# Attention and two expert stages on one core: attention's PSUM and the opening order rearranged

## The chip, the core and the metric

The kernel runs on one core of a Trainium2 chip. The engines of the core that matter here are TensorE (PE in the profile; PEld is its weight load), VectorE (DVE), ScalarE (ACT), GpSimd (POOL) and the queue engine SyncE (SP). [...] The metric is the device time of one execution, in microseconds (us).

## What is computed

Attention over 4 batches, 8 heads and 768 positions, in chunks of 32 queries that see 8 memory keys and a window of their neighbours; then a mixture of 8 experts whose weights come from a balanced softmax over all 3072 tokens; then one more feed-forward stage.

```python
def _attn_ref(q, k, v, mem_k, mem_v):            # q, k, v: (4, 8, 768, 64)
    for c in range(S // 32):                     # keys c*32-16 .. c*32+40, cut at 0 and S
        scores = scale * q_c @ concat(mem_k, k_ctx).T
        a = exp(scores - max(scores)); a = a / (sum(a) + 1e-9)
        out[c] = a @ concat(mem_v, v_ctx)

def _moe_ref(x, w_gate, w1, w2):                 # x: (3072, 512), w1: (8, 512, 1024)
    P = exp(x @ w_gate - max)
    for _ in range(8):
        P /= P.sum(1) + 1e-9; P /= P.sum(0) + 1e-9; P *= N / E
    return sum(P[:, e] * (relu(x @ w1[e]) @ w2[e]) for e in range(8))

def _moe2_ref(x, w_in, w_out):                   # w_in: (512, 2048)
    return relu(x @ w_in) ** 2 @ w_out
```

## The kernel before, in words

Every fp32 operand of a product is scaled by a power of two and split into a high and a low fp16 half; a product is then three fp16 products (low by high, high by low, high by high). ACT makes the high half, DVE or POOL the low one by a subtraction.

Attention works on 32 tiles of 96 queries. One tile goes through these steps (functions `a_...`): load k, v, q into one of three buffers `raw`; `a_scale`, `a_all`, `a_row_max`, `a_spread`, `a_scale2` find the largest magnitude of each of the three and make scales of it (L247 to L271; two tiny products on PE in between); `a_split` and `a_split_lo` make the halves (L300 on ACT, L305 on DVE); `a_tqk` turns q and k by a transposing DMA on SP's queue (L310); `a_scores` computes the scores (L329, L341), `a_max` their row maxima (L350 to L355, DVE); `a_mt`, `a_mtc` turn the maxima (L361 on PE, L367 on ACT); `a_st` computes the scores a second time, turned and with the maximum taken off (L378, L381); `a_exp` (L390), `a_asplit` (L396), `a_asplit_lo` (L402, POOL) make the weights; `a_av` (L411 to L419) multiplies with v; `a_norm` (L428 to L431, DVE) divides; `a_xsplit`, `a_xsplit_lo` split the result and `a_tx` turns it into `xt` by transposing DMAs (L455). `setup_less` builds three mask tables `less` on ACT (L1462, L1465), which the scores need.

Expert 0 runs in between: token blocks of 128, 128 and then 256 tokens; for a block `l1_mm` computes x @ w1 (L784 to L786, a group of 24 products for each quarter f of the hidden columns), `l1_relu` on ACT (L791) and `l1_lo` on DVE (L796) make the halves of the result, `l2_part` multiplies with w2 (L1291 to L1293), `l2_acc` stores (L1299). Its weights are loaded by SP (`w1_load0` L581, `w2_load0` L587), searched for their maximum by DVE (L590), scaled and split by ACT (L652, L655) and POOL (L658). The gate products (`gate` L465, L472 and `gate_out` L482) run once for each 128 tokens. After the last tile and gate `open_post` opens the pools of the later stages; experts 1 to 7 and the last stage follow with products at L930 and L1291.

PSUM during attention: four one-bank buffers `sc` (two for each of the two score steps), two banks `ps` for the experts, and one two-bank tile `avb`. `avb` holds the output of `a_av` in both banks and, behind it in the second bank (`mmb`), the small results of `a_all`, `a_spread`, `a_mt` and `gate`.

The order of the work on every engine is computed when the program is built: the class `Plan` takes tasks with an engine, a cost, a priority and what they wait for, and always places the task that can start first (ties by priority). Its rings stand for buffers; `lane` stands for 8 semaphores that all DMAs share in turn, so that a DMA waits for the one eight before it. Each engine then runs its list strictly in that order.

Of the kernel before, what the change touches and what calls it, by code (L numbers as in the profile page):

```python
# [7 lines left out]
F32 = mybir.dt.float32  # L8
# [13 lines left out]
    "hi": 1.85, "lo": 2.25, "tqk": 3.1, "scores": 0.95, "max": 1.65, "mt": 0.12, "mtc": 0.25,  # L22
    "st": 1.0, "exp": 1.05, "ahi": 0.85, "alo": 1.7, "av": 0.8, "norm": 1.05, "xhi": 0.65,
    "xlo": 0.7, "tx": 1.25,
}
LAND = {"load": 1.8, "tqk": 4.4, "tx": 1.7, "w": 2.5}
SLACK = 0.6
MOVE = {"load": 3.6, "tqk": 4.5, "tx": 1.5, "w1": 1.5, "w2": 1.3}
X2 = [[[0, 3, 5, 8], [9, 10, 14, 17], [1, 4, 13, 15, 10, 15, 21]], [[0, 3, 5, 8], [9, 10, 14,
# [24 lines left out]
def tile_attention_moe_moe2(  # L54
# [92 lines left out]
    ident16 = ap_.tile([TQ, TQ], F16, name="ident16")  # L147
# [11 lines left out]
    avb = psa.tile([P, 2, 512], F32, name="avb")  # L159
    mmb = avb[:, 1, 4 * VP:]  # L160
# [47 lines left out]
    def a_load(i):  # L208
# [3 lines left out]
        dq = nc.sync if i in (0, 2) else nc.scalar  # L212
        hd = lambda ap: ap.rearrange("p (h d) -> p h d", h=H)
        for t, src, mem in ((1, k, mem_k), (2, v, mem_v)):
            lo, hi = s0 - LEFT, s0 + TQ + RIGHT
# [5 lines left out]
            if c0 > lo:  # L221
# [9 lines left out]
            if mem_in.get((raw_of(i), t)) != b:  # L231
# [3 lines left out]
                )  # L235
        dq.dma_start(
# [6 lines left out]

    def a_scale(i):
        raw = raws[raw_of(i)]
        mx = ap_.tile([P, 3], F32, tag="amx", name="amx", bufs=2)
        nc.vector.tensor_reduce(mx, raw, AX.X, ALU.max, apply_absolute_value=True)  # L247
        st[i, "amx"] = mx

    def a_all(i):  # L250

        p = mmb[0:3, 0:P]
# [8 lines left out]
    def a_spread(i):  # L261
        p = mmb[:, P:P + 3]
# [5 lines left out]
    def a_scale2(i):  # L268
        sc, inv = pow2(st.pop((i, "gm")), 3, T_QKV, sml, "a")
        sce = sml.tile([P, 1], F32, tag="sce", name="sce", bufs=6)  # L270
        nc.vector.scalar_tensor_tensor(  # L271
            sce, inv[:, 0:1], 1.0 / float(D) ** 0.5, inv[:, 1:2], ALU.mult, ALU.mult
        )
        st[i, "sc"], st[i, "sce"], st[i, "inv"] = sc, sce, inv

    def a_invx(i):
        inv = st.pop((i, "inv"))
        t0 = i * TQ
        while t0 < (i + 1) * TQ:
# [3 lines left out]
            nc.gpsimd.tensor_copy(invx[p0:p0 + n, c:c + 1], inv[p0:p0 + n, 2:3])  # L283
# [28 lines left out]

    def qk_of(qkT, h):
# [10 lines left out]
    def a_scores(i):  # L324

        qkT = st[i, "qkT"]
        scs = [psa.tile([TQ, 4, P], F32, tag="sc", name="sc", bufs=4) for u in range(2)]
# [15 lines left out]
        st[i, "scp"] = scs  # L343

    def a_max(i):

        scs = st.pop((i, "scp"))
        mx = ap_.tile([TQ, 2, 4], F32, tag="smx", name="smx", bufs=2)
        for g in range(2):
# [3 lines left out]
        m = mx.rearrange("p g h -> p (g h)").unsqueeze(1).to_broadcast([TQ, 2, H])  # L353
# [3 lines left out]
    def a_mt(i):  # L357

        p = mmb[0:MR, P + 4:P + 4 + TQ]
        m16 = m16s[i % 2].rearrange("p g c -> p (g c)")[:, 0:MR]  # L360
        nc.tensor.matmul(p, lhsT=m16, rhs=ident16, start=True, stop=True)  # L361
# [8 lines left out]
    def a_st(i):  # L370

        qkT, mt = st.pop((i, "qkT")), st.pop((i, "mt"))
        scs = [psa.tile([P, 4, TQ], F32, tag="sc", name="sct", bufs=4) for u in range(2)]
# [10 lines left out]
        st[i, "scp"] = scs  # L384

    def a_exp(i):
        scs, sce = st.pop((i, "scp")), st.pop((i, "sce"))
        e = ap_.tile([P, H, TQ], F32, tag="e", name="e")
        for g in range(2):
            nc.scalar.activation(e[:, 4 * g:4 * g + 4, :], scs[g], AF.Exp, scale=sce)  # L390
# [13 lines left out]
    def a_av(i):  # L404
        aT = st.pop((i, "aT"))
        v16 = v16s[i % NV]
        o = avb[0:TQ]
# [53 lines left out]
    def gate(t):  # L461
        b, c = divmod(t * P, BLK)
        lgp = mmb[:, 228:228 + 2 * E].rearrange("p (s e) -> p s e", s=2)
        for kk in range(KD):
            nc.tensor.matmul(  # L465
                lgp.rearrange("p s e -> p (s e)"),
                lhsT=xt[b][:, 0, kk, c:c + P],
                rhs=g16[:, kk].rearrange("p s e -> p (s e)"),
                start=(kk == 0),
                stop=False,  # L470
            )
            nc.tensor.matmul(  # L472
# [1490 lines left out]
```

## Time and profile before

| | us |
|---|---|
| median of 3 runs (lowest, highest) | 2533.57 (2528.68, 2533.63) |
| the profiled execution, its own time | 2531.32 |
| its span from first to last instruction | 2529.5 |
| PE busy, share of the span | 2407.2, 95% |
| DVE busy | 1871.1, 74% |

The profile divides the span into 40 slices of 63 us. PE's busy share reads 2 tenths in the first slice, 6 in the second and 9 in each of the others. A row of the timeline gives the start, the duration and the instruction, and in brackets how long the engine stood idle before it and what ended that. A row of a table of stretches gives, for each engine, its busy time in the stretch.

### The profile page before, as it was taken

What the parts mean: (1) busy time and instruction counts of PE and PEld (TensorE: products, weight loads), DVE (VectorE), ACT (ScalarE), POOL (GpSimd) and SP (SyncE); (2) the same over time, 40 slices, a digit from 0 to 9 for tenths busy, and PEclk for the clock granted to TensorE, in tenths of its full rate; (3) what the DMA queues carried; (4) which work ended last, traced back from release to release, by engine and by line L of the source; (5) the groups of instructions that cost most, each with busy time, mean ns of one, the idle gap of its engine ahead of it and who ended that gap; (6) DMA issues with size and microseconds to landing.
All of it is one profiled execution on the core that took longest, in us unless ns stands there. A gap on an engine that the chain in (4) does not pass through costs nothing.

```text
span 2529.5 us, 54257 instructions
## 1 busy us (share of the span) xinstructions
PE 2407.2 (95%) x22483; PEld 2015.5 (80%) x22483; DVE 1871.1 (74%) x2759; ACT 1337.6 (53%) x2294; POOL 1327.3 (52%) x1108
## 2 busy tenths in 40 slices
PE   2699999999999999999999999999999999999999
PEld 1566666657678888888888888888888878888888
DVE  7788764856577887888788788977858987666655
ACT  4455543423345564555556555555656657666453
POOL 2221211443545574675567467555746677866444
PEclk9999999999999999999999999999999999999999
DMA  8699774223353445445344544533333466553211
GB/s 173 100 144 145 120 109 90 80 76 111 112 198 117 142 123 189 131 145 188 116 142 132 176 134 142 188 124 101 119 119 112 141 165 161 164 168 113 91 64 48
DMA packets 358656, 329.53 MB, mean 130 GB/s; under 512 B 237320, under 2 KB 292104, under 8 KB 351752
## 3 DMA queue, kind: packets, MB, share of 16 engines
q1 hardware_dynamic: 274792, 305.08, 41.5%
q10 hardware_dynamic: 83616, 20.98, 5.3%
q8 instruction: 176, 2.88, 0.5%
q14 instruction: 72, 0.59, 0.1%
HBM read 214.84 MB, written 77.07 MB: 115 GB/s over the span
## 4 chain that ended last, share of the span: by engine, by line
PE 82%; DVE 12%; ACT 2%; DMA 2%; issue 1%; POOL 1%; ACTq 0%; SPq 0%; DVEq 0%; POOLq 0%
PE pbA L930 36%; PE pbE L930 18%; PE pbB L930 8%; PE pb L930 4%; PE py L1291 3%; PE py L1292 3%; PE py L1293 3%; PE ph L784 1%; PE ph L786 1%; PE ph L785 1%; DVE hp L1128 1%; DVE acc L1241 1%; PE sc L341 1%; DVE smx L350 1%; PE sct L378 1%
## 5 line engine op out<-in xcount | busy, mean ns | idle before, releaser
L930 PEld LDWEIGHTS <-wb 128*128 128x128 f16 x5184 | 507.4, 98 | 68.0 <-issue 7.6
L930 PEld LDWEIGHTS <-hp 128*128 128x128 f16 x4608 | 450.9, 98 | 58.0 <-DVE hp L1128 3.0
L930 PEld LDWEIGHTS <-wx 128*128 128x128 f16 x3888 | 380.8, 98 | 52.8 <-issue 8.0
L930 PEld LDWEIGHTS <-xt 128*128 128x128 f16 x3456 | 338.2, 98 | 48.3 <-DVE xt L1128 7.3
L930 PE MATMUL pbA<-w2p,hp 128*128 128x256 f16 x2304 | 291.4, 273 | 3.7 <-DVE hp L1128 1.9
L930 PE MATMUL pbA<-S,wb 128*128 128x256 f16 x2304 | 283.3, 273 | 6.2 <-ACT u L1058 2.0
L930 PE MATMUL pbE<-xt,wx 128*128 128x256 f16 x2304 | 284.1, 273 | 4.7 <-DVE u L1063 3.8
L1058 ACT ACTIVATE u<-pbA 128x512 f32<-128x512 f32 x180 | 106.5, 592 | 186.5 <-PE pbA L930 186.5
L402 POOL TENSOR_TENSOR aT<-e,aT 128x768 f16<-128x768 f32 x32 | 53.0, 1657 | 228.9 <-ACT aT L396 152.0
L930 PE MATMUL pbA<-w2p,xt 128*128 128x256 f16 x1152 | 157.1, 273 | 0.0
L930 PE MATMUL pbE<-xt,hp 128*128 128x256 f16 x1140 | 156.6, 274 | 0.0
L930 PE MATMUL pbE<-xt,xt 128*128 128x256 f16 x1140 | 156.2, 273 | 0.2 <-POOL xt L1128 0.2
L1291 PE MATMUL py<-w2p,hp 128*128 128x512 f16 x384 | 147.6, 384 | 7.6 <-DVE hp L921 6.0
L1058 ACT ACTIVATE xt<-pbA 128x512 f32<-128x512 f32 x147 | 86.6, 592 | 128.0 <-PE pbA L930 128.0
L1128 POOL TENSOR_TENSOR hp<-u,hp 128x512 f16<-128x512 f32 x86 | 115.2, 1339 | 65.0 <-ACT hp L1121 65.0
L1292 PE MATMUL py<-w2p,hp 128*128 128x512 f16 x384 | 147.1, 383 | 0.0
L1293 PE MATMUL py<-w2p,hp 128*128 128x512 f16 x384 | 146.9, 383 | 0.0
L930 PE MATMUL pbA<-S,wx 128*128 128x256 f16 x1152 | 141.4, 273 | 2.3 <-ACT xt L1058 0.9
L930 PE MATMUL pbA<-xt,wb 128*128 128x256 f16 x1152 | 141.4, 273 | 0.0
L930 PE MATMUL pbB<-xt,wb 128*128 128x256 f16 x1152 | 141.4, 273 | 0.0
L1063 DVE TENSOR_TENSOR u<-pbE,u 128x512 f32<-128x512 f32 x100 | 68.6, 686 | 92.4 <-ACT u L1058 55.1
L1128 POOL TENSOR_TENSOR xt<-u,xt 128x512 f16<-128x512 f32 x72 | 94.8, 1325 | 54.9 <-ACT xt L1121 54.9
(367 smaller groups left out, 5710.6 us busy)
## 6 DMA issues: line engine op xcount, KB each, us to landing
wst<-in_moe_w_dram SPq DMA_DIRECT2D x80, 512.0 KB
xt<-xdr SPq DMA_DIRECT2D x40, 1024.0 KB
S<-sdr SPq DMA_DIRECT2D x126, 256.0 KB
w2d<-wst SPq DMA_DIRECT2D x32, 512.0 KB
w2p<-w2d SPq DMA_DIRECT2D x32, 512.0 KB
wst<-in_moe_w_dram SPq DMA_DIRECT2D x56, 256.0 KB
xdr<-xt SPq DMA_DIRECT2D x12, 1024.0 KB
w2d<-tw SPq DMA_DIRECT2D x32, 384.0 KB
```

The lines of the kernel that those rows point to most:

```text
L341: nc.tensor.matmul(scs[u][:, hh, :], lhsT=q_, rhs=k_, start=False, stop=(s == 2 and hh == 3))
L350: nc.vector.tensor_reduce(mx[:, g], scs[g], AX.X, ALU.max)
L378: nc.tensor.matmul(scs[u][:, hh, :], lhsT=k_, rhs=q_, start=(s == 0 and hh == 0), stop=False)
L402: nc.gpsimd.tensor_tensor(aT[:, 1], st.pop((i, "e")), aT[:, 0], ALU.subtract)
L784: nc.tensor.matmul(p[:, r], lhsT=w[:, 1], rhs=xh, start=first, stop=False)
L930: nc.tensor.matmul(p[:, r], lhsT=w[:, ws], rhs=x[:, xs], start=a, stop=z, skip_group_check=onto)
L1058: nc.scalar.activation(t, p, AF.Copy, scale=sc)
L1063: nc.vector.tensor_tensor(t, p, t, ALU.add)
L1128: eng.tensor_tensor(d[:, 1], t, d[:, 0], ALU.subtract)
L1291: nc.tensor.matmul(p, lhsT=h[:, 1], rhs=w[:, 0], start=first, stop=False)
L1292: nc.tensor.matmul(p, lhsT=h[:, 0], rhs=w[:, 1], start=False, stop=False)
L1293: nc.tensor.matmul(p, lhsT=h[:, 0], rhs=w[:, 0], start=False, stop=last)
```

## The change

- **PSUM by use.** `avb` goes. The scale steps get a bank of their own (`pa`), the row maxima and their turned form another (`pb`), and the two score steps, the output of `a_av`, the gate products and the new transposes share a ring of two two-bank buffers (`wide`, tag `sc`). The row maximum and the exponential become one instruction each over both banks; the scale steps and the maxima stay in PSUM while they are worked on.
- **Tiles 0 and 1** are turned by products with an identity on PE and copied out by ACT or DVE (`a_tq1`, `a_tqc`; 16 products of 128 columns a tile); the results x of tiles 0, 1 and 2 likewise (`a_tx1`, `a_txc`; 8 products a tile).
- **Loads.** Tiles 0 to 3 are loaded by SP's queue, except v of tile 0, which goes to ACT's; tile 1's loads stand ahead of most of the w1 loads. The rows of tile 0 ahead of position 0 are set to zero by DVE in place of being loaded.
- **Weights of expert 0**: one scaled ACT instruction and one DVE instruction in place of two on ACT and one on POOL; the L1 groups need only two of the four w1 pieces each, and run f = 0, 2, 1, 3.
- **Gates**: six groups of four token tiles; the gate weights are prepared after tile 16, the maxima of expert 1's w2 after tile 22.
- `a_invx` moves from POOL to ACT.
- **The plan** adds to a task's possible start an offset for its step (`AHEAD`) and a share of its priority by engine (`AGE`), and places the smallest sum first. Costs are renewed.

```diff
+AHEAD = {
+    "join": -0.54, "setup_less": 2.51, "a_all": -0.23, "a_row_max": -0.45, "a_spread": -0.08,
...
-        dq = nc.sync if i in (0, 2) else nc.scalar
+        dq = nc.sync if i < 4 else nc.scalar
...
+            if i == 0 and t == 2:
+                dq = nc.scalar
...
+    def wide(nm, rows=P):
+        return psa.tile([rows, 2, 512], F32, tag="sc", name=nm, bufs=2)
...
-        p = mmb[0:3, 0:P]
+        st[i, "pa"] = pa = psa.tile([P, 256], F32, tag="pa", name="pa", bufs=1)
+        p = pa[0:3, 0:P]
...
+        nc.vector.tensor_scalar(
+            eb.bitcast(I32), eb.bitcast(I32), EXP_MASK, None, ALU.bitwise_and)
+        nc.vector.tensor_scalar(inv, eb, 2.0 ** -100, 2.0 ** -T_QKV, ALU.max, ALU.mult)
+        nc.vector.tensor_scalar(eb, eb, 2.0 ** -100, None, ALU.max)
+        nc.vector.tensor_scalar(
+            sc.bitcast(I32), eb.bitcast(I32), -1.0, float((254 + T_QKV) << 23), ALU.mult, ALU.add)
...
-            nc.gpsimd.tensor_copy(invx[p0:p0 + n, c:c + 1], inv[p0:p0 + n, 2:3])
+            nc.scalar.activation(invx[p0:p0 + n, c:c + 1], inv[p0:p0 + n, 2:3], AF.Copy)
...
+    def a_tq1(i, m):
+        p = wide("sqt")
+        for c in range(8):
+            n = 8 * (c // 4) + 4 * m + c % 4
+            nc.tensor.matmul(
+                p[:, c // 4, c % 4 * P:(c % 4 + 1) * P], lhsT=st[i, "qk"][:, n * P:(n + 1) * P],
+                rhs=ident16, start=True, stop=True)
+        st[i, "tq", m] = p
...
-            nc.vector.tensor_reduce(mx[:, g], scs[g], AX.X, ALU.max)
+        st[i, "pb"] = pb = psa.tile([P, 128], F32, tag="pb", name="pb", bufs=1)
+        mx = pb[0:TQ, TQ:TQ + H]
+        nc.vector.tensor_reduce(mx, scs.rearrange("p g (h n) -> p (g h) n", h=4), AX.X, ALU.max)
...
-        o = avb[0:TQ]
+        o = wide("av", TQ)
...
+    def w_hi0(n, d):
+        nc.scalar.activation(flat(d[:, 0]), flat(stage0[n]), AF.Copy, scale=wsc[0, n // 4][0])
+
+    def w_lod0(n, d):
+        nc.vector.scalar_tensor_tensor(
+            flat(d[:, 1]), flat(stage0[n]), wsc[0, n // 4][0], flat(d[:, 0]), ALU.mult, ALU.subtract)
...
+        fill(raws[0][0:LEFT, 1:3, :], 0.0)
...
+                        key = t + AHEAD.get(fn.__name__, 0.0) + AGE.get(eng, 0.0) * pri / 100
...
-        plan = Plan({"lane": 8, "lgp": 1, "pmax": 1, "pall": 1, "pmt": 1, "sc": 4, "av": 1, "ps": 2})
+        plan = Plan({"lane": 8, "pa": 1, "pb": 1, "sc": 2, "ps": 2})
...
+            if blk and (c0 + n0) % (NGP * P) == 0:
+                t = (c0 + n0) // (NGP * P) - 1
+                G[t] = add("PE", 0.36 * NGP, 9000, gate, t, after=x_in + [W["gp"]], ring=("sc", 1))
...
-                w_in_ = [W["lo", n] for n in range(4)]
+                w_in_ = [W["lo", 2 * (f % 2) + n] for n in range(2)]
```

The order that the plans give, at three places. First ACT at the start of the program, before (`raw_162` and `raw_163` are the buffers of tiles 0 and 1, `qk` and `v` the high halves):

```order
L217 DMA raw_163<-in_k_dram 120x8x64
L233 DMA raw_163<-in_mem_k_dram 8x8x64
L217 DMA raw_163<-in_v_dram 120x8x64
L233 DMA raw_163<-in_mem_v_dram 8x8x64
L236 DMA raw_163<-in_q_dram 96x8x64
L1462 ACTIVATE less<-heads 83x1024
L1465 ACTIVATE less<-maskr 3x1024 x2
L300 ACTIVATE qk_298<-raw_162,asc 128x512 x2
L300 ACTIVATE v_0_165<-raw_162,asc 128x8x64
```

and the same engine now, from its first instruction (`sqt` is q and k turned by PE, in PSUM):

```order
L235 DMA raw_162<-in_v_dram 104x8x64
L251 DMA raw_162<-in_mem_v_dram 8x8x64
L1560 ACT_TABLE_LOAD
L1560 ACTIVATE less<-heads 83x1024
L1563 ACTIVATE less<-maskr 3x1024 x2
L360 ACTIVATE qk_293<-raw_162,asc 128x512 x2
L360 ACTIVATE v_0_164<-raw_162,asc 128x8x64
L317 ACTIVATE invx<-ainv 96x1
L381 ACTIVATE qkT<-sqt 128x2x512
```

All three mask tables and tile 1's five loads stood ahead of tile 0's high halves; now one table does, the other two stand behind, and tile 1's loads are on SP's queue.

Second, the low halves of expert 0's w1 (`wb`). Before, on POOL:

```order
L283 COPY invx<-ainv 96x1
L283 COPY invx<-ainv 32x1
L283 COPY invx<-ainv 64x1
L658 TENSOR_TENSOR wb_84<-acc_78,wb_84 128x1024
L658 TENSOR_TENSOR wb_86<-acc_78,wb_86 128x1024
L658 TENSOR_TENSOR wb_85<-acc_79,wb_85 128x1024
L658 TENSOR_TENSOR wb_87<-acc_79,wb_87 128x1024
L402 TENSOR_TENSOR aT<-e,aT 128x768
```

and now on DVE, between steps of tiles 2, 5 and 6 (`x_941` is the low half of tile 2's result, `qk_893` that of tile 5):

```order
L270 TENSOR_REDUCE amx<-raw_162 128x3
L517 TENSOR_SCALAR rs<-av 96x8
L518 RECIPROCAL rs<-rs 96x8
L520 TENSOR_TENSOR acc_83<-av,rs 96x512
L285 TENSOR_REDUCE ag<-pa 3x1
L754 SCALAR_TENSOR_TENSOR wb_84<-acc_78,w0sc,wb_84 128x1024
L534 TENSOR_TENSOR x_941<-acc_83,x_941 96x512
L339 SCALAR_TENSOR_TENSOR qk_893<-acc_83,asc,qk_893 128x512 x2
```

The four subtractions moved from POOL, where they ran ahead of the first tile's weights, to DVE, the first behind tile 2's division and the others further down.

Third, DVE behind the row maxima of tile 7, up to tile 6's division (`rs`). Before:

```order
L350 TENSOR_REDUCE smx<-sc 96x4 x2
L354 CAST m_1_159<-smx 96x2x8
L355 TENSOR_TENSOR m_1_159<-smx,m_1_159 96x2x8
L190 TENSOR_SCALAR aeb<-avb 128x3
L191 TENSOR_SCALAR ainv<-aeb 128x3
L194 TENSOR_SCALAR asc<-ainv 128x3
L271 SCALAR_TENSOR_TENSOR sce<-ainv 128x1
L590 TENSOR_REDUCE wmx<-acc_82 128x1
L247 TENSOR_REDUCE amx<-raw_163 128x3
L428 TENSOR_SCALAR rs<-avb 96x8
```

and now, from the fourth instruction behind the same maxima (`qk_1649` and `v_0_164` are tile 8's low halves, `pa` the scale steps in PSUM):

```order
L285 TENSOR_REDUCE ag<-pa 3x1
L339 SCALAR_TENSOR_TENSOR qk_1649<-acc_83,asc,qk_1649 128x512 x2
L339 SCALAR_TENSOR_TENSOR v_0_164<-acc_83,asc,v_0_164 128x8x64
L270 TENSOR_REDUCE amx<-raw_163 128x3
L300 TENSOR_SCALAR pa<-pa 128x3
L302 TENSOR_SCALAR ainv<-pa 128x3
L303 TENSOR_SCALAR pa<-pa 128x3
L304 TENSOR_SCALAR asc<-pa 128x3
L306 SCALAR_TENSOR_TENSOR sce<-pa,ainv 128x1
L285 TENSOR_REDUCE ag<-pa 3x1
L517 TENSOR_SCALAR rs<-av 96x8
```

Tile 8's low halves moved in between the maxima and the division, and the search of expert 1's w2 (`acc_82`) has gone from there.

## Rows read from the trace of the kernel before

**Rows 1.** The page: span, and PE's busy tenths in 40 slices.
```profile
span 2529.5 us, 54257 instructions
...
PE   2699999999999999999999999999999999999999
```
**Rows 2.** Stretches: length, busy (count) of PE, PEld, DVE, ACT, POOL, granted clock, DMA.
```profile
0.00:87.40 87.40, 26.79 (x352) 20.17 (x353) 66.88 (x139) 46.96 (x60) 31.36 (x51) 1.00 0.77 147
...
34.50:87.40 52.90, 25.09 (x345) 19.44 (x345) 45.84 (x85) 30.15 (x43) 25.09 (x19) 1.00 0.63 118
87.40:113.00 25.60, 17.71 (x209) 14.50 (x209) 11.38 (x22) 7.93 (x18) 2.12 (x4) 0.87 0.77 111
113.00:444.00 331.00, 312.50 (x3941) 218.68 (x3941) 236.99 (x503) 154.30 (x297) 62.35 (x78) 0.99 0.76 121
```
**Rows 3.** Timeline (start, us, instruction): tile 0 from the fills to its scores.
```profile
0.96 1.03 DVE L1421 MEMSET raw<- 32x512 f32 x2 [0.96 <-PEq L1947]
...
9.13 2.13 ACT L1465 ACTIVATE less<-maskr 3x1024 bf16<-3x1024 bf16 x2 [1.55 <-POOL maskr L1459]
...
18.77 1.33 ACT L300 ACTIVATE qk<-raw,asc 128x512 f16<-128x512 f32 x2
...
22.46 9.52 SPq L310 DMA_TRANSPOSE qkT<-qk  x2
...
34.55 0.66 PE L329 MATMUL sc<-less,onehot 3*96 3x512 bf16 x2
```
**Rows 4.** DVE groups by form, 0 to 88 us: count, busy us, mean ns, idle before.
```profile
L590 DVE TENSOR_REDUCE wmx<-acc 128x1 f32<-128x1024 f32 x8 | 9.4, 1204 | 0.0
L247 DVE TENSOR_REDUCE amx<-raw 128x3 f32<-128x1536 f32 x5 | 8.7, 1747 | 10.9 <-DMA raw<-in_q_dram 10.9
L350 DVE TENSOR_REDUCE smx<-sc 96x4 f32<-96x512 f32 x10 | 6.4, 677 | 2.2 <-PE sc L341 2.2
L305 DVE SCALAR_TENSOR_TENSOR qk<-raw,asc,qk 128x512 f16<-128x512 f32 x8 | 5.6, 744 | 0.0
...
L431 DVE TENSOR_TENSOR acc<-avb,rs 96x512 f32<-96x512 f32 x3 | 2.1, 686 | 0.1
```
**Rows 5.** Timeline: POOL's w1 halves, DVE's small steps beside and after; page's POOL group.
```profile
34.69 8.44 POOL L658 TENSOR_TENSOR wb<-acc,wb 128x1024 f16<-128x1024 f32 x4 [9.53 <-issue]
34.92 1.93 DVE L191 TENSOR_SCALAR ainv<-aeb 128x3 int32<-128x3 int32 x1
...
43.09 0.14 DVE L190 TENSOR_SCALAR aeb<-avb 128x3 int32<-128x3 int32 x1
43.34 0.17 DVE L191 TENSOR_SCALAR ainv<-aeb 128x3 int32<-128x3 int32 x1
...
L402 POOL TENSOR_TENSOR aT<-e,aT 128x768 f16<-128x768 f32 x32 | 53.0, 1657 | 228.9 <-ACT aT L396 152.0
```
**Rows 6.** Timeline: PE's two long stops around the first L1 groups, and ACT's.
```profile
87.38 0.31 PE L361 MATMUL avb<-ident,m 96*83 96x96 f16 x1 [4.67 <-DVE m L355]
...
105.23 0.18 ACT L482 ACTIVATE lg<-avb 128x16 f32<-128x16 f32 x1 [8.36 <-DMA acc<-in_v_dram]
...
105.47 0.21 PE L411 MATMUL avb<-v,aT 128*96 128x65 f16 x1 [6.90 <-ACT lg L482]
```
**Rows 7.** Timeline of PE: 12 L1 products, 24 later ones, tile 5's scores.
```profile
87.48 0.31 PE L784 MATMUL ph<-xt,wb 128*128 128x128 f16 x1
...
88.65 0.31 PE L786 MATMUL ph<-xt,wb 128*128 128x128 f16 x1
...
93.71 0.22 PE L784 MATMUL ph<-xt,wb 128*128 128x128 f16 x1
...
94.99 0.22 PE L786 MATMUL ph<-xt,wb 128*128 128x128 f16 x1
...
113.47 0.87 PE L341 MATMUL sc<-qkT 64*96 64x128 f16 x24
```
**Rows 8.** Timeline: end of one tile's last product with v, and its division on DVE.
```profile
193.27 0.21 PE L419 MATMUL avb<-v,aT 128*96 128x65 f16 x1
...
202.39 0.69 DVE L431 TENSOR_TENSOR acc<-avb,rs 96x512 f32<-96x512 f32 x1
```

More of the change, by code (lines that the diff above doesn't have):

```diff
@@ L235, in a_load @@
                 )
+        dq = nc.sync if i == 0 else dq
         dq.dma_start(
@@ L326, in a_scores @@
         qkT = st[i, "qkT"]
-        scs = [psa.tile([TQ, 4, P], F32, tag="sc", name="sc", bufs=4) for u in range(2)]
+        both = wide("sc", TQ)
+        scs = [both[:, u].rearrange("p (h n) -> p h n", h=4) for u in range(2)]
         for g, sc in zip(GRP, scs):
@@ L372, in a_st @@
         qkT, mt = st.pop((i, "qkT")), st.pop((i, "mt"))
-        scs = [psa.tile([P, 4, TQ], F32, tag="sc", name="sct", bufs=4) for u in range(2)]
+        both = wide("sct")
+        scs = [both[:, u, 0:4 * TQ].rearrange("p (h n) -> p h n", h=4) for u in range(2)]
         for s in range(3):
@@ L1575, in tile_attention_moe_moe2, with join, s_hi0, s_lo0 @@
         }
-        RING = {"row": ("pmax", 1), "all": ("pall", 1), "mt": ("pmt", 1), "scores": ("sc", 2),
-                "st": ("sc", 2), "av": ("av", 1), "tqk": ("lane", 1)}
-        FREE = {"row": ["row_mx"], "all": ["scale"], "mt": ["mtc"], "scores": ["max", "max"],
-                "st": ["exp", "exp"], "av": ["norm"]}
+        RING = {"row": ("pa", 1), "max": ("pb", 1), "scores": ("sc", 1), "st": ("sc", 1), "av": ("sc", 1),
+                "tqk": ("lane", 1)}
+        FREE = {"row": ["scale"], "max": ["mtc"], "scores": ["max"], "st": ["exp"], "av": ["norm"]}
         T = {}
-        LS = [add("ACT", 3.2, 5 + 100 * mv, setup_less, mv) for mv in range(3)]
+        def join():
+            pass
+        def s_hi0():
+            s_hi(*st["sf", 0])
+        def s_lo0():
+            s_lo(*st.pop(("sf", 0)))
+        S0 = add(None, 0.0, -999, join, land=6.0)
+        LS = [add("ACT", 3.2, 5 + 100 * mv, setup_less, mv, after=[S0]) for mv in range(3)]
         for i in range(NA):
@@ L1586, in tile_attention_moe_moe2 @@
                 eng = ENG[n]
-                if n == "load" and i in (0, 2):
+                if n == "load" and i < 4:
                     eng = "SP"
@@ new lines, in tile_attention_moe_moe2 @@
+                if n == "tx" and i < PX:
+                    lasts = []
+                    for m in range(2):
+                        tq = add("PE", 0.45, pri, a_tx1, i, m, after=after if m else [T[i, "xhi"]] + after[1:],
+                                 ring=("sc", 1))
+                        act = m == 0 or i > 0
+                        cp = add("ACT" if act else "DVE", 0.5, pri - 1, a_txc, i, m, act, after=[tq])
+                        holds(tq, cp)
+                        lasts.append(cp)
+                    T[i, "tx"] = add(None, 0.0, pri - 1, join, after=lasts, land=0.2)
+                    continue
```

216 lines of the change are left out of this document (145 added, 71 removed), and 3 rows, old and new, of the table AHEAD.

## Prediction

> **What bounds the kernel now.** I read the page first. PE is busy 95% of a span of 2529.5 us, and its slices read 2 and 6 tenths at the start and 9 from then on [rows 1]. So the kernel is bound by PE except in its opening, and since the change touches nothing behind attention and expert 0, its gain must come out of that opening. The table of stretches says how much is there: up to 87.4 us PE works 26.8, from 87.4 to 113 it works 17.7 of 25.6 at a mean clock of 0.87, and from 113 to 444, where attention and expert 0 run side by side, it works 312.5 of 331 [rows 2]. In the last of these only 18.5 us are open; in the first two 68.5 are, though part of that is the latency of the first tiles and cannot go.
>
> What holds the opening? From 34.5 to 87.4 DVE is busy 45.8 of 52.9 us and ACT 30.2 [rows 2]: DVE works its list without a gap worth naming, and the first L1 product, at 87.48, starts behind a small product that had waited 4.67 us for DVE [rows 6, 7]. Ahead of that the timeline of tile 0 shows a chain without load: mask tables on ACT until 11.26, more of them behind tile 1's loads, the high halves only at 18.77, a transposing DMA issued at 22.46, scores only at 34.55 [rows 3]. Behind it there is one long stop: PE idles 6.90 us up to 105.47 for a gate copy on ACT, which had stood 8.36 us behind a load that waited for its DMA semaphore [rows 6].
>
> **The change, part by part.**
>
> *Tile 0 to its scores.* The new fill of 16 x 1024 stands first on DVE; two fills of 32 x 512 take 1.03 us together, and so will this one [rows 3]. POOL's masks, and with them the one table that is still ahead of tile 0, end 1.0 us later: 9.13 + 2.13 + 1.0 = 12.3. High halves of k and q 1.33 (to 13.6), the three low halves on DVE 0.74 each behind the first of them (to 15.0). Then DVE's list has tile 1's maximum, 1.75 (to 16.7), ahead of the copy of the turned low halves. No row shows that copy; a reduction over 512 columns of PSUM takes 0.68, so 1024 cost about 1.3 [rows 4]: 18.0. PE's 16 turning products, 0.106 each as 128-column products at the lower of PE's two clock levels [rows 7], lie beside DVE's work. This needs tile 1 to have landed by 15; its loads are issued right behind tile 0's and one w1 piece. Scores of tile 0 at 18, not 34.55. If tile 1 lands at its old 19, the copy ends at 22: bounds 17 and 22.
>
> *From there to the first L1 product.* It needs two pieces of w1 and x of tiles 0 and 1. In the new list of DVE the low half of the second piece stands behind these, each with its row's duration [rows 4, 5]: 7 searches of weights 1.20 = 8.4; 6 maxima of inputs 1.75 = 10.5; 5 row maxima, two halves of 0.68 and two small steps = 8.5; 15 low halves 0.74 = 11.2; 30 scale steps 0.17 = 5.1; 4 divisions 0.69 + 0.35 = 4.2; 3 low halves of x 0.69 = 2.1; some 21 small steps 4.4; one copy 0.5; the two w1 halves, each twice a 0.74 = 3.0. Sum 57.9. Durations overlap a little from one to the next, and DVE also waits: in the old stretch 7.1 of 52.9 were not busy [rows 2]. I let the two nearly cancel: 18 + 58 + 1 = 77, bounds 74 and 84, against 87.48. PE's list ahead of it is by then through the turned scores of tile 4, and its waits fit into this.
>
> Not in that sum any more: the stretched steps. One scale step took 1.93 us while POOL ran its four w1 halves, and 0.17 undisturbed [rows 5]. POOL no longer has them, and the scale steps now read PSUM, as the one of 0.14 does. [...]
>
> *From the first L1 to the dense stretch.* PE's new list has 168 L1 products of 128 columns, two score steps, one turned score step and two products with v ahead of the first product with w2. Products start 0.106 apart for the first 6 us and 0.056 from 93.71 on [rows 7]: 57 x 0.106 + 111 x 0.056 = 12.3, and about 1.2 for each of the five attention steps, 18 in all: 95. DVE's list has 17 us of work from the second w1 half to the first w2 half and 22 to the fourth: 94 and 99. So products with w2 start at 95 and may wait for DVE up to 4 us. Before, tile 5's scores start at 113.47 with 96 L1 products of 128 columns and 15 w2 products of 512 issued [rows 7]; the new list at 95 is ahead of that point by 1536 columns or 0.6 us of expert work and by two score steps, one turned one and one product with v, about 4. The 6.90 stop is not repeated: the gates leave this place. Gain: 113.5 + 4.6 - 95 = 23, less 3 for DVE: **20**. From the bounds: 10 to 26.
>
> *The rest, 113 to 444.* Zero, and here is its cover. DVE gets 8 weight halves (12 us, half of them above) and one more scale step a tile (5 us), and is busy 237 of 331 [rows 2]. ACT gets POOL's copies of scales and loses eight passes over weights; it is busy 154 of 331. The gate products are the same 192, in six lumps. The gate weights and expert 1's maxima go behind tiles 16 and 22, where DVE has room, and expert 0's token tile 19 is what waits for the latter. The waits through `avb` in that stretch can give back at most what is open, 18.5. Against that the ring of two wide buffers is tighter, see below. Sum: 2531.32 - 20 = **2511**. The profiled execution lies inside the runs (2528.68 to 2533.63), so I give the same number for the median.
>
> **The rivals.**
>
> *DVE late once more.* w1's and w2's low halves now run on DVE with two operands in SBUF, while POOL subtracts for the attention weights, 1.66 us each [rows 5]. If DVE and POOL block each other where they meet, the six POOL instructions ahead of the first w2 product put up to 6 x 1.66 = 10 us into DVE's chain. The gain falls to 10: **2521**. For it: the 1.93 us step beside POOL. Against it: the plan lets these two kinds of work not overlap. It decides from about half of the meetings. [...]
>
> *The ring of two.* Scores, turned scores and products with v share two buffers, and PE works in order. In the new list the step two places after a product with v comes 2.6 to 5 us of PE work later; it must find that buffer divided and free. Before, the division ended 9.6 us after the product (193.48 to 203.08), at no cost, since that buffer was waited for by nobody else until the next one [rows 8]. If divisions lag so that half of the 27 later tiles stop PE for 3 us, that is 42 us: 2531 - 20 + 42 = **2553**, slower. It decides from 0.75 us per tile. Against it: behind the maxima of the next tile the new list does about 5 us of work before the division, and PE's product with v itself comes about that late.
>
> *Given back later.* The plan may trade the opening for holes: PE's open time from 113 to 444 would grow from 18.5 to 38, for example because loads on ACT's queue stand behind their DMA semaphores as at 105.23, with exponentials queued behind them. Then nothing is left: **2531**. For it: those waits are unchanged in kind. Against it: it takes three such stops.
>
> *More than that.* If the waits of the dense stretch halve too, 9 us more: **2501**.
>
> **How the numbers follow.** Forecast 0.55 (own range 2503 to 2519); DVE late 0.17 (2519 to 2528); more 0.09 (2494 to 2503); given back 0.07 (2528 to 2539); the ring 0.12 (2540 to 2565). A measurement of this kernel can tell about 0.2%, 5 us, from no change. Faster by more: 0.55 + 0.17 + 0.09 = 0.81; within: 0.07; slower: 0.12. Half of the fourth case and most of the third belong to a range of eight in ten: 2499 to 2531.
>
> **What would show it.** Right: tile 0's scores near 18, the first L1 product near 77 and the first w2 product near 95; no scale step above 0.3 us; the stretch from there to the end of expert 0 with no more open PE time than before, ending near 424 where it ended at 444. Wrong: tile 0's scores after 22 (loads), weight halves on DVE stretched above 2 us (POOL), stops of PE in front of score steps with a division as releaser (the ring), one stop of several us behind a load on ACT (given back). The forecast fails as a whole if PE's open time before the first w2 product does not shrink.

## The result, and the profile after

The changed kernel takes 2487.8 us (median of 4 runs, 2485.1 to 2489.4) against 2533.5 before (4 runs, 2528.7 to 2533.6): 0.982 of the time, interval 0.981 to 0.984. That is 46 us less; I had forecast 22 less, and 2487.8 lies below my range (2499 to 2531).

The page of the changed kernel, its span and PE's busy tenths in 40 slices, answers to [rows 1]:

```profile
span 2486.0 us, 54260 instructions
...
PE   4999999899999999999999999999999989999999
```

The first slice went from 2 to 4, the second from 6 to 9. The stretches answer to [rows 2], same columns: to the first L1 product, from there to the first product with w2, from there to the first product of expert 1 (the dense stretch below), and the rest. Open time of PE is a stretch's length less PE's busy time.

```profile
0.00:71.40 71.40, 37.65 (x466) 28.70 (x467) 63.20 (x150) 43.50 (x71) 12.30 (x33) 1.00 0.95 177
71.40:89.60 18.20, 16.56 (x304) 15.05 (x303) 17.99 (x32) 13.48 (x22) 3.66 (x2) 1.00 0.75 129
89.60:440.90 351.30, 344.22 (x4044) 235.49 (x4042) 264.96 (x557) 167.19 (x309) 67.57 (x51) 1.00 0.71 121
440.90:2486.00 2045.10, 2009.35 (x17734) 1736.89 (x17731) 1524.04 (x2035) 1115.48 (x1901) 1211.14 (x959) 1.00 0.41 132
```

By the prediction's own matching, the work issued at the first product with w2 now was issued at 113.5 + 4.6 = 118.1 before. The kernel before from there to its first product of expert 1, and behind it:

```profile
118.10:486.10 368.00, 347.84 (x4130) 241.39 (x4127) 267.80 (x571) 166.74 (x313) 81.33 (x96) 0.99 0.70 118
486.10:2529.50 2043.40, 2009.71 (x17731) 1735.90 (x17729) 1521.62 (x2019) 1114.51 (x1901) 1212.12 (x957) 0.99 0.41 132
```

So the opening gave 118.1 - 89.6 = 28.5 us (forecast 20), the dense stretch 368.0 - 351.3 = 16.7 (forecast 0), and what follows took 1.7 back: 43.5 between the two spans. In the dense stretch PE's open time fell from 20.2 to 7.1 us; the other 3.6 are busy time (347.8 to 344.2), at a granted clock of 1.00 where it was 0.99. The two points match only roughly: now 24 products of 512 columns more and 110 others fewer lie in the stretch. But the same 1056 L1 products of 256 columns stand in both, and their durations add up to 292.0 us before and 288.0 now.

What was open before? The waits of PE from 118.1 to 486.1 us in the kernel before (what waited, for whom; us in total, times, longest; rows under 0.3 left out):

```profile
PE ph L784 <- DVE hp L796: 5.1, 3, 3.8
PE avb L361 <- DVE aeb L190: 3.2, 2, 3.0
PE avb L253 <- DVE acc L431: 2.4, 5, 1.2
PE avb L361 <- ACT lg L482: 2.2, 1, 2.2
PE py L1291 <- DVE wma L630: 1.5, 1, 1.5
PE avb L465 <- ACT mt L367: 0.9, 1, 0.9
PE avb L411 <- ACT mt L367: 0.9, 1, 0.9
PE avb L263 <- DVE acc L431: 0.9, 1, 0.9
PE avb L253 <- ACT mt L367: 0.8, 2, 0.6
PE avb L361 <- DVE acc L431: 0.7, 1, 0.7
PE avb L253 <- ACT e L390: 0.7, 1, 0.7
PE avb L263 <- ACT lg L482: 0.5, 2, 0.3
```

All but the rows of `ph` and `py` are waits through `avb`, 13.4 us with one row left out, and in hardly any of them does the product read the result that it waits for. L361 turns a tile's maxima; it waits for DVE to read another tile's scale steps (3.2 us), or for ACT to copy gates (2.2 us), and these lie in other columns of the same bank: in these rows the waits go by the tile and not by the columns. The same view of the changed kernel, 89.6 to 440.9:

```profile
PE pa L280 <- DVE amx L270: 1.6, 2, 1.2
PE ph L881 <- DVE hp L893: 1.6, 3, 1.2
PE av L508 <- POOL aT L491: 1.5, 1, 1.5
PE pb L449 <- DVE m L443: 1.1, 2, 0.9
PE sc L417 <- DVE acc L520: 0.5, 1, 0.5
```

Here `pa`, `av` and `pb` wait for their own input, `ph` for its own buffer to be read out, `sc` for a division to free a buffer of the ring. So the 13.1 us of open time that went are a balance: 13.4 through `avb` became 4.7 through `pa`, `pb` and `av` (two rows of 0.3 and 0.2 not shown), and expert 0's waits (`ph`, `py`) fell from 6.6 to 1.6. That the first is due to the split tile is a matter for the experiments; what made the second smaller was not tested by itself.

### The profile page after: what moved, and what is told of

Read it like the earlier page. It is cut to its first block, busy times and chain, and to the rows that moved or that the text cites. A ratio compares the mean times of both kernels' runs of the same rounds, so it can differ in the third digit from the quotient of the medians.

```text
span 2486.0 us, 54260 instructions
## 1 busy us (share of the span) xinstructions
PE 2407.8 (97%) x22539; PEld 2016.1 (81%) x22539; DVE 1870.2 (75%) x2772; ACT 1339.6 (54%) x2300; POOL 1294.7 (52%) x1044
## 4 chain that ended last, share of the span: by engine, by line
PE 77%; DVE 8%; ACT 2%; POOL 1%; DMA 1%; issue 1%; SPq 0%; ACTq 0%; DVEq 0%; POOLq 0%
PE pbA L1027 36%; PE pbE L1027 18%; PE pbB L1027 9%; PE pb L1027 4%; PE py L1388 2%; PE py L1390 2%; PE py L1389 2%; DVE hp L1225 1%; DVE acc L1338 1%; PE ph L881 1%; PE ph L882 1%; PE ph L883 1%; DVE xt L1225 0%; DMA qkT<-qk 0%; DVE u L1036 0%
## 5 line engine op out<-in xcount | busy, mean ns | idle before, releaser
L1160 DVE TENSOR_TENSOR u<-pbE,u 128x512 f32<-128x512 f32 x100 | 68.6, 686 | 94.5 <-ACT u L1155 54.8
```

What stands on the lines that cost most here:

```text
L1160: nc.vector.tensor_tensor(t, p, t, ALU.add)
```

## The experiments

The change names three kinds of thing: parts that alter what an instruction does or where its data lies, the order, and both. So most experiments come in two forms. With **the list kept**, the plan is told nothing, only bodies of functions change, and every other instruction keeps its place. With **a new list**, the plan computes the order again for the altered tasks (e2, e3, e5 to e8 and e12 too). All times are medians; before ran again beside each group of experiments (2531.1 to 2533.0), the changed kernel did not. So a difference of 2 or 3 us from its 2487.8 is within what the groups differ by. "To expert 1" is the first product of expert 1, with PE's open and busy time up to it, and "behind" what follows.

| kernel | time | first L1 | to expert 1 | open | busy | behind |
|---|---|---|---|---|---|---|
| before | 2533.5 | 87.5 | 486.1 | 88.7 | 397.4 | 2043.4 |
| changed | 2487.8 | 71.4 | 440.9 | 42.5 | 398.4 | 2045.1 |
| e1 changed, one shared tile, list kept | 2515.9 | 83.1 | 472.5 | 68.6 | 403.9 | 2043.0 |
| e5 before, split alone | 2526.4 | 84.3 | 483.5 | 83.0 | 400.5 | 2038.9 |
| e2 changed, no offsets | 2507.0 | 50.4 | 465.3 | 61.1 | 404.2 | 2040.0 |
| e11 the same, shared tile, list kept | 2523.2 | 51.5 | 487.9 | 76.9 | 411.0 | 2037.6 |
| e12 before, offsets alone | 2550.8 | 75.4 | 493.9 | 94.0 | 399.9 | 2054.7 |
| e4 changed, no turning, new list | 2504.2 | 72.7 | 458.5 | 61.4 | 397.1 | 2043.3 |
| e10 changed, no turning, list kept | 2501.8 | 85.6 | 454.8 | 62.5 | 392.2 | 2045.4 |
| e7 changed, w1 halves on POOL, new list | 2532.1 | 59.7 | 472.9 | 63.9 | 409.0 | 2058.7 |
| e9 changed, w1 halves on POOL, list kept | 2490.1 | 73.4 | 444.6 | 43.1 | 401.6 | 2044.5 |
| e3 changed, gates early, one by one | 2517.0 | 71.3 | 460.2 | 51.9 | 408.3 | 2055.0 |
| e8 changed, gates early, in fours | 2518.2 | 71.2 | 457.9 | 54.7 | 403.2 | 2058.5 |
| e6 before, gates late alone | 2538.4 | 89.6 | 496.4 | 91.6 | 404.8 | 2042.2 |
| e13 three parts undone, list kept | 2532.0 | 93.6 | 487.5 | 89.0 | 398.6 | 2044.4 |
| e14 changed, DVE late once | 2495.6 | 71.5 | 449.3 | 49.1 | 400.2 | 2042.9 |
| e15 changed, last colsum later | 2488.4 | 71.4 | 439.0 | 39.9 | 399.1 | 2044.4 |

### The shared tile: e1, e5, e11

```diff
+    avb = psa.tile([P, 2, 512], F32, name="avb")
+    mmb = avb[:, 1, 4 * VP:]
-        st[i, "pa"] = pa = psa.tile([P, 256], F32, tag="pa", name="pa", bufs=1)
+        st[i, "pa"] = pa = mmb[:, 0:P + 4]
-        st[i, "pb"] = pb = psa.tile([P, 128], F32, tag="pb", name="pb", bufs=1)
+        st[i, "pb"] = pb = mmb[:, P + 4:P + 4 + TQ + H]
-        o = wide("av", TQ)
+        o = avb[0:TQ]
```

> The changed kernel with its PSUM as before in one respect: the output of the product with v, the scale steps, the row maxima and their turned form share one two-bank tile again; the list of every engine stays the changed kernel's. At stake are the 16.6 us that the changed kernel gained from its first product with w2 (89.6 us) to the first product of expert 1 (440.8 us): 351.2 us where the same work took 367.8 us before, 7.1 us of them open on PE where 20.2 were. Sharing theory: the waits of PE through that one tile come back, some 10 to 16 us between 90 and 440 and a few in the opening: 2500 to 2508. Order theory (the offsets of the plan keep every result ready in time, whatever tile it lies in): 2486 to 2492, and PE's open time from 89.6 to the end of expert 0 stays below 10 us.

It cost 28 us, more than the sharing theory asked for. Its opening and its dense stretch, then its waits of PE in the latter:

```profile
0.00:83.10 83.10, 37.05 (x465) 28.74 (x465) 65.15 (x152) 44.46 (x71) 12.30 (x33) 1.00 0.84 152
102.00:472.50 370.50, 349.44 (x4043) 238.58 (x4041) 267.25 (x558) 167.50 (x309) 68.93 (x52) 0.99 0.67 115
```
```profile
PE avb L292 <- DVE m L445: 7.9, 8, 2.7
PE avb L502 <- DVE ag L287: 2.6, 4, 1.5
PE avb L451 <- DVE acc L522: 2.3, 2, 1.2
```

With the same list the dense stretch is open for 21.1 us again, as before the change (20.2), 19.3 of them through `avb`, and the waits are of the old kind: L292 spreads a scale and waits for DVE to split another step's maxima. (The waits of `ph` and `py` do not come back: 1.5 us.) And 11.7 us more stand ahead of the first L1 product, which I had not put down to the tile at all.

e5 is the kernel before with pa, pb and the ring of two wide buffers, and nothing else (in the diff of the change the lines on `avb`, `mmb`, `wide`, and the plan's rings).

> The kernel before with one part of the change alone: the PSUM split by use (a bank for the scale steps, a bank for the turned maxima, a ring of two wide buffers for scores, turned scores, products with v and gates; the plan's rings to match). Everything else is the kernel before. Putting the shared tile back into the changed kernel cost 28 us there, 11.7 of them ahead of the first L1 product. Sharing theory: on the old order too the split is worth most of that, 2505 to 2518, and the open time of PE from the first product with w2 to expert 1 falls from 20.2 us to below 12. Rival: the split pays only with the plan's offsets, which let steps follow each other closely enough to meet in one tile: 2525 to 2534. The ring rival of the prediction would give over 2540.

It gains only 6.6 us (ratio 0.998, 0.997 to 0.999): the rival. PE is open for 19.2 us from its first product with w2 to expert 1, where before had 20.2. None of it goes through `avb` any more; now it waits for DVE's row maxima, its own input (five waits, 7.1), a gate copy (2.38), a copy of expert 0's results on ACT (3.87):

```profile
PE pb L364 <- DVE m L358: 7.1, 5, 2.7
PE ph L788 <- ACT acc L1303: 3.9, 1, 3.9
```

So the 13.4 us that the view of before shows through `avb` were not to be had by the split alone: with the old rule of order, other waits took their place.

e11 is e2 (below) with the lines of e1.

> The run without offsets (2507 us) with its list kept, and scales, maxima and product with v in one shared PSUM tile again. With the offsets sharing cost 28 us; on the old order the split was worth 6.6. If sharing costs by itself: 2525 to 2536. If it costs only where the offsets pack the steps of neighbouring tiles close: 2508 to 2516.

Plus 16 us against e2, outside both ranges, and all of it open time of the dense stretch (43.2 us against e2's 26.7): under a third list the same tile costs between what it does under the other two. The price of the sharing depends on the list. That it is how closely the list packs neighbouring tiles is my reading; no run varies that by itself.

### The order by itself: e2, e12

```diff
-AHEAD = {"join": -0.54, ...}
-AGE = {...}
+AHEAD = {}
+AGE = {}
```

> The changed kernel with all of the plan's offsets empty, so that the plan places the task that can start first, as before; the PSUM, the turning on PE, the loads and the gates are the changed kernel's. Sharing theory: the dense stretch keeps most of its 16.6 us, at most 5 us are lost there, and what is lost in the opening is under 8 us: 2488 to 2500. Order theory: the dense stretch opens to 20 us again: 2503 to 2515.

19 us slower, by the order theory's numbers. It starts expert 0 far earlier (first L1 at 50.4, first product with w2 at 63.2) and is later at expert 1: the time of the first product says little. Opening and dense stretch:

```profile
0.00:50.40 50.40, 17.38 (x223) 13.55 (x224) 41.78 (x97) 32.21 (x45) 9.78 (x31) 0.84 0.84 169
63.20:465.20 402.00, 375.35 (x4410) 262.74 (x4407) 299.32 (x654) 186.25 (x345) 73.89 (x55) 0.95 0.69 118
```

26.7 us are open in the latter, and the mean granted clock is 0.95.

e12 puts the same table and its term in the plan into the kernel before.

> The kernel before with the plan's offsets alone (the steps they name that it has; PSUM, turning, loads, gates and weight halves as before). If the offsets carry the gain by themselves: 2505 to 2520. If they pay only together with the parts that they were chosen for: 2528 to 2560, with open PE time from the first product with w2 to expert 1 not below the 20.2 us of before.

19 us slower than before (ratio 1.008, 1.007 to 1.010), as the second theory has it. The order is worth nothing without the parts it was made for.

### Turning on PE: e4, e10

```diff
-    PQ, PX = 2, 3
+    PQ, PX = 0, 0
```

> The changed kernel with tiles 0 and 1 (q and k) and x of tiles 0 to 2 turned by transposing DMAs again. By the prediction's first step the scores of tile 0 move from 18.1 to about 31 us (low halves at 15.5, the old transposing DMA took 9.5 us, 12 us from issue to scores). If what follows is a DVE list without room, the first L1 product moves by as much, from 71.4 to about 83, and the time to 2497 to 2502. Rival: DVE fills the gap with searches of weights that are ahead of it anyway, so that half is lost: first L1 at 76 to 78, 2492 to 2496.

Neither: the scores come at 37.8, the first L1 product hardly later (72.7), and yet 16 us are lost, all of them behind it. So the list was kept in e10, where `a_tq1` and `a_tx1` do nothing and the last copy issues the DMA:

```diff
     def a_tqc(i, m, act):
+        if m:
+            a_tqk(i)
     def a_txc(i, m, act):
+        if m:
+            a_tx(i)
```

> The changed kernel with q, k of tiles 0 and 1 and x of tiles 0 to 2 turned by transposing DMAs, issued where the last copy of the turned tile stood; the plan is told nothing, so every other instruction keeps its place. The run e4 let the plan make a new list: scores of tile 0 at 37.8, first L1 at 72.7, 2504 us. With the list kept, DVE's list cannot fill the gap: scores of tile 0 near 30 and all behind it later by 10 to 13, tile 1's by some more: first L1 at 82 to 92, 2498 to 2510. If turning on PE hardly matters (the list has room for it), first L1 before 76 and under 2493.

Inside the bounds: first L1 at 85.6, 14 us slower, all in the opening, and 6.0 us open in the dense stretch, much as in the changed kernel (7.1):

```profile
104.50:454.80 350.30, 344.29 (x4044) 235.16 (x4042) 264.37 (x557) 167.36 (x309) 69.08 (x52) 1.00 0.69 122
```

### w1's low halves on POOL: e7, e9

```diff
-                if m in (0, 1, 2, 3, 4, 5, 6, 7):
+                if m > 3:
```

> The changed kernel with the low halves of expert 0's w1 and w2 by POOL again (two ACT instructions and one POOL instruction each, as before); DVE loses eight instructions of 1.27 us. If POOL's work stretches DVE's steps, as the 1.93 us step beside POOL in the kernel before says: scale steps above 0.3 us while these run, first L1 at 73 to 78, 2493 to 2502. If DVE's list alone bounds the opening, two halves less of it ahead of the first L1 product: 69 us, 2483 to 2487.

(The edit moves the four halves of w1, not all eight.) Neither theory: first L1 at 59.7, and 44 us slower, so that the whole gain is gone.

```profile
73.70:472.80 399.10, 368.36 (x4279) 254.99 (x4277) 273.80 (x577) 178.89 (x332) 68.04 (x51) 0.95 0.67 114
472.80:2531.60 2058.80, 2013.93 (x17737) 1737.91 (x17735) 1531.47 (x2055) 1117.36 (x1902) 1216.05 (x960) 0.99 0.41 132
```

Up to expert 1, 21 us are open time and 11 busy time, with a mean granted clock of 0.95 in the dense stretch; 14 are lost behind expert 0, where PE waits for weights and column sums. Is that POOL or the list? e9 makes the same move inside `w_hi0` and `w_lod0`:

```diff
     def w_lod0(n, d):
+        if n < 4:
+            w_lo0(n, d)
+            return
```

> The changed kernel with the low halves of expert 0's four w1 pieces (w2's stay on DVE) by POOL, two ACT instructions in front of each, but the plan is told nothing: every other instruction keeps its place in its engine's list. The run e7 moved the same four halves (its expectation spoke of eight) and let the plan make a new list: 2532 us, although its first L1 product came at 59.7 us. List theory: what e7 lost came from the other list, with loads, x and maxima late behind it; with the list kept the price is POOL's 2.13 us in place of 1.27 and one more ACT instruction, 2488 to 2497. POOL theory: DVE and POOL hold each other up, 2510 or more here too, with scale steps of DVE above 0.3 us.

2490.1: the list theory. The move itself costs 2 us, no more than the groups of runs differ by, the other list 42. In the trace of the changed kernel 17 scale steps ran beside one of POOL's subtractions (four of them from 152.67 on) and took 0.15 to 0.17, as the others did. They read PSUM now, into which all of PE's products go here. Before, four small steps with operands in SBUF, where `asc`, `smx` and `m` lie, ran beside POOL's halves [rows 5] and took 1.93, 2.05, 0.63 and 2.09 us in place of 0.17 to 0.18 each:

```profile
36.88 2.05 DVE L194 TENSOR_SCALAR asc<-ainv 128x3 int32<-128x3 int32 x1
40.41 0.63 DVE L354 CAST m<-smx 96x16 f16<-96x16 f32 x1
41.08 2.09 DVE L355 TENSOR_TENSOR m<-smx,m 96x16 f16<-96x16 f32 x1
```

That is 6.0 us of DVE's opening. It suggests why the place of the halves matters so little in e9: the small steps that stood beside them have moved to PSUM.

### Gates: e3, e8, e6

```diff
-        g0 = add("DVE", 0.6, 2500, gate_max, after=[W["gl"], W["sc", 1], T[16, "mx"]])
+        g0 = add("DVE", 0.6, 400, gate_max, after=[W["gl"], W["sc", 1]])
```

(and priority 400 in the four tasks behind it; e3 also has `NGP = 1`.)

> The changed kernel with the gates as before: one group for each 128 tokens, as soon as its x is there, and the gate weights prepared at their old priority instead of after tile 16; the gate products stay in the ring of wide buffers. If the stop of 6.90 us behind a gate copy that I took as part of the opening's gain comes from early gates: PE waits for a gate copy on ACT between 90 and 130 us, 2493 to 2499. If that stop came from the shared tile, through which the next step had to wait for the copy: no PE stop above 2 us there, 2486 to 2492.

> The changed kernel with one half of the earlier run with early gates: the gate weights are prepared at their old priority, the gates still run in six groups of four token tiles. If it was the early preparation (its load and its steps on DVE fall into 90 to 110 us and move tile loads ahead on ACT's queue) that cost 29 us: a stop of PE above 3 us between 95 and 115 with the clock at half behind it, 2503 to 2517. If it was the 24 single gates: 2486 to 2493.

Both lose 29 to 30 us (e3 more than either of its theories has, e8 1 us more than its first), so grouping is not what counts. PE stops at 105 (in e8 at 104, for 4.12 us) for DVE's maximum, which stood behind x from ACT, and ACT had stood 5.56 us behind a tile load that waited for its DMA semaphore. e3, PE at that stop, then three stretches between 104 and 118 us:

```profile
105.06 0.22 PE L280 MATMUL pa<-ident,amx 128*3 128x128 bf16 x1 [4.16 <-DVE amx L270]
```
```profile
104.00:106.00 2.00, 0.94 (x3) 0.36 (x4) 1.69 (x3) 0.49 (x1) 0.00 (x0) 0.81 0.88 116
106.00:108.00 2.00, 2.00 (x20) 0.96 (x20) 1.58 (x3) 0.00 (x0) 0.00 (x0) 0.50 0.18 33
...
112.00:118.00 6.00, 5.34 (x49) 3.70 (x43) 5.03 (x13) 3.64 (x6) 1.64 (x1) 0.51 1.30 197
```

Behind the stop PE works at half its clock from 106 to 108 and again from 112 to 118, after more and shorter stops (0.88, 0.48, 0.66). Whether early gates cost this by themselves or by the new list stays open: no form with the list kept was run.

e6 is the opposite on the kernel before: gate weights after tile 16, maxima of expert 1 after tile 22.

> The kernel before with another part alone: the gate weights prepared after tile 16 and the maxima of expert 1's w2 after tile 22, so that no gate runs near 100 us. The prediction's step put the stop of 6.90 us at 105 down to the gate copy on ACT and took it as gone with the gates. Gates theory: that stop goes, 2522 to 2527. Load theory (the copy was only the first thing behind the load that waited 8.36 us for its DMA semaphore; in the run with early gates the stop came back at 105 behind x on ACT, which stood 5.56 us behind such a load): another instruction of ACT takes its place, a stop of 4 us or more stays between 95 and 115, 2529 to 2535.

The stop of [rows 6] does go, the first product with w2 comes at 100.2 instead of 108.9, and yet the kernel is 5 us slower (ratio 1.003, 1.002 to 1.004), so neither theory holds: from there to expert 1, 31.2 us are open, 21 of them through `avb`, at a clock of 0.96. The 9 us were given back, and more.

### Do the parts add? e13

The edits of e1, e10 and e9 together, list kept.

> The changed kernel with three parts undone at once and every list kept: one shared PSUM tile (28 us by itself), transposing DMAs for tiles 0 to 2 (14), w1's low halves on POOL (2). If they add: 2528 to 2536, all of the gain, and the list by itself is worth nothing without them. If they overlap (the opening waits for the latest of them, not for their sum): 2510 to 2524. If they compound: over 2540.

2532.0, no different from before (ratio 1.000, 0.999 to 1.001). They add: 28.2 + 14.0 + 2.3 = 44.5, and 44.3 were lost. (Each taken against the before of its own group, the three are 30.6, 16.2 and 4.5, together 51, and 44.8 were lost; so they add to within a few us.) Its opening and dense stretch:

```profile
0.00:93.60 93.60, 30.77 (x410) 23.89 (x411) 63.25 (x148) 41.55 (x66) 17.48 (x35) 1.00 0.82 153
113.00:487.50 374.50, 349.93 (x4044) 238.57 (x4042) 264.73 (x555) 171.93 (x313) 76.31 (x56) 0.99 0.63 114
```

24.6 us are open in the latter. The list, the loads and the gates, which stay changed here, are together worth nothing without these three.

### The price of one delay: e14

```diff
+            for _ in range(6 if i == 12 else 1):
                 nc.vector.tensor_reduce(mx, raw, AX.X, ALU.max, apply_absolute_value=True)
```

> The changed kernel, lists kept, with tile 12's maximum searched six times instead of once: 8.7 us more of DVE at about 122 us, in a place where PE runs without a stop and DVE is busy 83% of the time behind it. If the dense stretch has slack: 2488 to 2491, no stop above 2 us. If PE pays what DVE is late by and no more: one or two stops of 3 to 6 us, 2491 to 2495, clock 1.00. If a stop costs more than its length: the clock falls behind it and the time is 2496 to 2505.

One stop, and the clock behind it:

```profile
133.92 0.26 PE L281 MATMUL pa<-ident,amx 128*3 128x128 bf16 x1 [7.48 <-DVE amx L271]
```
```profile
130.00:140.00 10.00, 6.08 (x43) 2.97 (x44) 8.53 (x14) 0.84 (x2) 0.00 (x0) 0.66 0.10 20
140.00:150.00 10.00, 10.00 (x127) 6.52 (x126) 7.83 (x19) 5.33 (x11) 1.65 (x1) 1.00 0.95 143
```

7.8 us slower by the medians (the four runs lie between 2492.1 and 2501.0), for 8.7 us of DVE. Between the last two theories: the stop is longer than I expected, the clock does fall (0.66 over the 10 us that hold the end of the stop; products with w2 start 0.43 us apart up to 136.22 and 0.22 from 136.90 on), and PE's busy time to expert 1 grows by 1.8 us. PE's stretch without stops has almost no slack: of the 8.7 us, 7.48 reach PE, though DVE has some room there (in the changed kernel busy 23.5 of the 28 us from 122 to 150).

### A better kernel? e15

```diff
-                       land={"load": 2.6, "start": 0.6}.get(step.__name__, 0.0 if mm else 2.5))
+                       land={"load": 2.6, "start": 0.6}.get(step.__name__, 0.0 if mm else (9 if n == 16 else 2.5)))
```

> The changed kernel with one number changed: the plan is told that the last column sum of the gate balance is ready 6.5 us later than it assumed, so that PE's list has this product behind eight products groups with w2 of expert 1 instead of ahead of them (ACT, POOL and SP keep their lists, DVE changes in 27 rows). PE stood 7.06 us in front of it in the changed kernel. If that stop is a loss by itself: 2479 to 2484. If those products with w2 then wait for DVE in its place, as DVE's steps there are stretched (1.88 us for one that takes 0.36 elsewhere, beside POOL's subtractions of w2): 2485 to 2490.

The rival. The 7.06 us go, and PE waits for w2 in their place, 2.6 + 4.8 us:

```profile
PE py L1389 <- POOL w2p L827: 4.8, 2, 3.1
PE py L1388 <- ACT w2p L824: 2.6, 1, 2.6
```

2488.4 against 2487.8 is no difference. No version was found that beats the changed kernel.

## Why the prediction was wrong, step by step

**Tile 0 to its scores: right.** The copy on DVE ended at 18.07 (forecast 18.0), and the scores of q and k started at 18.13 (their mask product ran ahead, at 17.20). The answer to [rows 3]:

```profile
18.13 1.09 PE L429 MATMUL sc<-qkT 64*96 64x128 f16 x16 [0.28 <-DVE qkT L383]
```

The copy took 1.21 (taken 1.3). That turning pays, and only in the opening, e10 shows: 14 us. The 0.106 us of a 128-column product I read as the lower clock level [rows 7], while the tables of stretches print 1.00 there. That 1.00 is no reading: the record of the granted clock in these traces begins only at 93.6 (before) and 73.7 (changed), and at just these times L1 products go from 0.106 to 0.056 us apart. No record states the clock up to there, but the rows fit the lower level: the record of the kernel before holds the values 1.00 and 0.50 and no other, and where it reads 0.50 (103.9 to 110.7) these products are 0.106 apart again (107.73 to 108.80).

**From there to the first L1 product: sum right, its reading wrong.** I had 57.9 us of DVE instructions; the groups of the stretch add up to 58.1. But they took 53.8:

```profile
18.07:71.86 53.79, 34.91 (x447) 26.94 (x447) 50.97 (x114) 34.35 (x60) 6.55 (x4) 1.00 0.93 166
```

The durations overlap by 58.1 - 51.0 = 7.1 us, and DVE was idle for 2.8. I took the idle 7.1 us of the old stretch to stand against "a little" overlap and let them cancel. But the old 45.8 was busy time, with the overlap already out; a sum of durations has to be brought down to that first. And part of the old idle time may have come from the tile: e1 puts 11.7 us back here by the tile alone. First L1 at 71.4, outside my bounds of 74 to 84.

Scale steps took 0.15 to 0.16 us from PSUM, where they had taken 0.17 from SBUF; the 1.93 did not come back.

**From the first L1 to the first product with w2: right in length** (18.2, forecast 18). The 3 us for DVE did not come; PE waited 0.93 and 0.66 for it. These 3 and the 5.4 by which this product came earlier than 95 are the opening's 28.5 in place of 20. That the 6.90 us stop goes with the gates was right on the old order too (e6), but there it brought nothing.

**The rest: the step that failed.** "Zero" measured 16.7; with the opening's error alone the time would have been inside the range. I had written that the waits through `avb` could give back at most the 18.5 us that were open, and then took none of it, with the tighter ring as the only reason against, which cost 0.5 (below). What the runs show in its place: under the changed list the shared tile holds 14 us of open time in this stretch (21.1 in e1, 7.1 in the changed kernel), and under e2's list 16.5 (e11). The other part is 3.6 us less busy time, at a clock of 1.00 in place of 0.99. The view of waits names this term, 13.4 us, without any new run, but it does not price it: on the old order the split took these waits away and freed 1.0 us (e5). The gain of this stretch needs the split and the new list together, and that the forecast did not have. My rival "more than that" had the right place, at 9 us and a chance of 0.09.

**The rivals.** The ring of two never stopped PE: no division stands among its releasers in the dense stretch but one of 0.5 us. DVE late through POOL: real, but met once before the first product with w2 (below). The trace of before already has a step with two inputs in SBUF that was stretched beside POOL: L355 above, with 2.09 us. Given back later: 1.7 us behind expert 0; but it is what became of e6.

**What I did not see at all:** the parts need each other. The split alone is worth 7 us, the offsets alone -19, late gates alone -5, and all parts together 46.

## What to carry to other kernels

Look for a shared buffer in the view of waits: sum the waits in which an instruction waits through it for a result that it does not read, in the full stretches too, where a few percent of open time over hundreds of us weigh here more than half as much as the opening. The sum says where to look; what it is worth depends on the order of the work (here 1.0 us of open time on one list, 14 on another) and takes a run. A part of a tuned kernel is measured with every engine's list kept; letting a planner make a new list mixes the part with the order (2 us of it for the turning, 42 for w1's halves), and an early start of the next stage tells nothing of its end. Bring a sum of row durations down to busy time (here 0.88 of it) before waits are added.

## What the runs showed of the hardware

DVE and POOL held each other up in some of the places where they met. In the changed kernel a pair of low halves of q and k (raw and its high half, both in SBUF) takes 1.40 us; at 73.66 it took 2.80, and DVE's second one ended 0.54 us behind POOL's subtraction:

```profile
74.32 2.13 DVE L339 SCALAR_TENSOR_TENSOR qk<-raw,asc,qk 128x512 f16<-128x512 f32 x1
74.22 1.69 POOL L491 TENSOR_TENSOR aT<-e,aT 128x768 f16<-128x768 f32 x1 [7.75 <-PE ph L883]
```

The same at expert 1: a product of `pm` with `sk_rs` takes 0.36 us at 443.81 and 1.88 at 462.59, beside POOL's subtractions of w2. The other way round, one of POOL's subtractions for the attention weights (100.99) took 3.23 us where 27 of the 32 took 1.64 to 1.65; DVE ran low halves of two SBUF inputs beside it (100.65 to 102.70), and these took 1.39 the pair and 0.73, no more than elsewhere. The scale steps from PSUM were not stretched (0.15 to 0.17 us beside POOL). Steps with a single tensor input in SBUF were stretched in the kernel before: L191, L194 and L354, as shown above (1.93, 2.05 and 0.63 us in place of 0.17 to 0.18).

Two stops cost PE more than themselves. Behind 4.16 us (e3) the granted clock read 0.50 from 106 to 108 us; behind 7.48 us (e14) it read 0.66 over 130 to 140, and products of 512 columns started 0.43 us apart up to 136.22 and 0.22 from 136.90 on. The one stop of e14 came with 1.8 us more busy time, and where stops followed one another (e2 and e7, mean granted clock 0.95 in the dense stretch) PE's busy time up to expert 1 was 6 and 11 us longer. The kernel before and e10 issue nearly the same products up to there (4754 and 4752), in 397.4 and 392.2 us of busy time; in their dense stretches the mean granted clock was 0.99 and 1.00.
